# Activation columns held apart by parity, group norm pieces on GpSimd, and constant products ahead of the first matmuls in a two-convolution residual block

## The chip, the cores and the metric

The kernel runs on one core of a Trainium2 chip. A core has a matrix engine (TensorE; PE in the profile, its weight loads PEld), a vector engine (DVE), an activation engine (ACT), a general engine (GpSimd; POOL) and a queue that only starts transfers (SP). They run side by side and wait for one another through semaphores. The metric is the device time of one execution in microseconds, as a median over runs; lower is better.

## The reference

A residual block of a diffusion model, on two samples of 512 channels and 64 x 64 pixels, in bf16:

```python
def gn(z, gamma, beta):                    # 4 groups of 128 channels
    zr = z.reshape(B, G, (C // G) * H * W)
    mu = zr.mean(-1).reshape(B, G, 1)
    var = ((zr - mu) ** 2).mean(-1).reshape(B, G, 1)
    zn = ((zr - mu) / jnp.sqrt(var + eps)).reshape(B, C, H, W)
    return zn * gamma.reshape(1, C, 1, 1) + beta.reshape(1, C, 1, 1)
h = conv3(_silu(gn(x, g1, be1)), w1)       # 3x3, zero padding
emb = _silu(t_emb) @ w_emb
h = h + emb.reshape(B, C, 1, 1)
h = conv3(_silu(gn(h, g2, be2)), w2)
return x + h
```

## The kernel before, in words

**Tiles.** The 512 channels are four tiles of 128 partitions (index ct for inputs, ot for outputs). The pixels are cut into four chunks of 32 rows: chunk 0 and 1 are sample 0, chunk 2 and 3 sample 1. Each of the two layers (convolutions) runs over the four chunks, and each chunk over the four output tiles: 32 sets in all (`one_set`; the last one is `final_set`).

**Winograd along rows.** A convolution is not done tap by tap. Groups of 4 output rows are made from 6 positions: `make_v` builds six sums V of the activation rows, `u_blocks` six sums U of the weights, TensorE multiplies them (`row_pair`, three column taps each, 512 wide, eight groups of 64 columns), and the products are put together again on ACT and DVE (the m1, w and y lines of `one_set`). For positions 0 and 5 most chunks (`is_col`: all of layer 1, chunks 1 to 3 of layer 0) use a transform along columns too: `make_v` makes sums and differences of neighbouring columns into V, for which even and odd columns are taken out of a row with a step of 2, and `col_pair` multiplies by `u_cols` weights, 256 wide; outputs of even and odd columns come out apart and are written into y with a step of 2. The last two chunks of layer 1 do this for positions 1 and 3 as well (`more_cols`, `more_pair`, `v_more`, `v_more_split`).

**A row of activations** (tile a_tmp) has 66 places: a zero, 64 columns, a zero. `silu_rows` writes it from x (layer 0) or from h, the first layer's output, which goes out to memory and comes back (layer 1).

**Statistics.** `first_stats` (sample 0) uses TensorE: products of x blocks with themselves (L943), whose diagonal DVE sums (L333, acc with ident), and column sums. `second_stats` (sample 1) uses sums on DVE (L985) and squares on ACT. Layer 1 takes sums that the output instructions of layer 0 leave behind (`stats2`). `norm` makes scale (sc) and bias (nb) of silu: a matmul with ones (L405) sums over partitions, DVE copies it out (L409), small DVE instructions make the variance, POOL adds eps (L419) and takes the power -1/2 (L423), small DVE instructions finish.

**Order.** Nothing is issued in the order of the text. Every instruction is a node of a plan (`_Plan`) with a cost, a landing time for transfers (PARAM_LAND for the parameters) and a due time. The planner lists the nodes many times with random changes and keeps the best order; each engine then runs its own list strictly in order. So a changed cost or node can move instructions everywhere. All helpers issue from one line each: `tt` (sum of two tensors on DVE) is L320, `ts` L325, `stt` L333, `act` L350, `dma` L368, transposes L389, matmuls of `groups` L645.

**Buffers that the steps touch.** acc0 to acc2 are three PSUM accumulators of 2 x 512; m1, mb, sd, w are single SBUF tiles for evictions and their sums; y0 to y2 hold finished chunks; Vbuf has two sets of four, one per chunk in turn. A finished y of layer 1 gets x added by an accumulating transfer from the POOL queue and goes out through SP; the last set loads x into y beforehand and sends its result as two halves from SP and ACT.

Of the kernel before, what the change touches and what calls it, by code (L numbers as in the profile page):

```python
# [24 lines left out]
class _Plan:  # L25
# [33 lines left out]
    def region(self, a):  # L59
        if isinstance(a, str):  # L60
            return a, 1
        m = self.mask(a.offset, tuple((d[0], d[1]) for d in list(a.ap)[1:]))
        bank = self.banks.get(a.tensor.name)
        if bank:
            m = sum(1 << i for i in range(8) if (m >> (i * bank)) & ((1 << bank) - 1))
        return a.tensor.name, m
# [124 lines left out]
def kernel(  # L191
# [36 lines left out]
    PARAM_LAND = 5.5  # L228
    LATE = 4.0
    DVE_SUMS = (1,)  # L230
# [31 lines left out]
    neg_half = sb([1], "neg_half", F32)  # L262
# [134 lines left out]
    def norm(layer, b, c0, n, me, ps=None):  # L397
# [15 lines left out]
        if n == 1:  # L413
            stt(nvar[:], mu, mu, ex, ALU.mult, ALU.add)
        else:
            tt(nvar[:], mu, mu, ALU.mult)
            tt(nvar[:], nvar[:], ex, ALU.add)
        ts(nvar[:], nvar[:], 0.0, op=ALU.min)
        pool(lambda: nc.gpsimd.tensor_scalar(out=rstd[:], in0=nvar[:], scalar1=-1.0, scalar2=EPS,  # L419
                                             op0=ALU.mult, op1=ALU.add), [nvar[:]], [rstd[:]])  # L420
        for i in range(n):
            r = rstd[:, i:i + 1]
            pool(lambda r=r: nc.gpsimd.tensor_tensor(out=r, in0=r, in1=neg_half[:], op=ALU.pow), [r, neg_half[:]], [r])  # L423
        sc, nb = sc_all[layer, b][:, c0:c0 + n], nb_all[layer, b][:, c0:c0 + n]
        tt(sc, rstd[:], gam(layer)[:, c0:c0 + n], ALU.mult)
        if layer == 1:
            tt(mu, mu, emb_sb[:, b, c0:c0 + n], ALU.add)
        if n == 1:
            stt(nb, mu, sc, bet(layer)[:, c0:c0 + n], ALU.mult, ALU.add)
        else:  # L430
            tt(nb, mu, sc, ALU.mult)
            tt(nb, nb, bet(layer)[:, c0:c0 + n], ALU.add)
# [92 lines left out]
    def v_more(V, X):  # L525
        rows = lambda kx, st: view(V, kx, [[2 * NI, 2], [WP, TR], [st, W // st]])
        dst = lambda o, n: view(X, o, [[n * TR, 2], [n, TR], [1, n]])
        tt(dst(0, W), rows(0, 1), rows(2, 1), ALU.subtract)
        tt(dst(4 * NC, W // 2), rows(1, 2), rows(2, 2), ALU.add)
        tt(dst(6 * NC, W // 2), rows(2, 2), rows(1, 2), ALU.subtract)  # L530
# [3 lines left out]
    def v_more_split(V, at, D):  # L534
        rows = lambda kx, st: view(at, kx, [[NI, 2], [WP, TR], [st, W // st]])
        tt(view(D, 0, [[W * TR, 2], [W, TR], [1, W]]), rows(0, 1), rows(2, 1), ALU.subtract)
        dst = lambda i: view(V, i * 2 * NI, [[NC, 2], [W // 2, TR], [1, W // 2]])
        tt(dst(0), rows(1, 2), rows(2, 2), ALU.add)
        tt(dst(1), rows(2, 2), rows(1, 2), ALU.subtract)

    def rhs_more_split(V, D, j, c):
        if c in (0, 3):
            return view(D, j * 2 * NC + (1 if c == 3 else 0), [[W, TR], [2, W // 2]])
        return view(V, (c - 1) * 2 * NI + j * NC, [[1, NC]])

# [3 lines left out]
    def rhs_row(V, pos, kx, col):  # L549
        i = pos - 1 if col else pos  # L550
        return view(V, i * NI + kx, [[WP, TR], [1, W]])

    def rhs_col(V, j, c, o=4 * NI):
        if c in (0, 3):
            return view(V, o + j * 2 * NC + (1 if c == 3 else 0), [[W, TR], [2, W // 2]])
        return view(V, o + (4 if c == 1 else 6) * NC + j * NC, [[1, NC]])

    def silu_rows(layer, b, ch, ct, res, at):
# [3 lines left out]
        for edge, r in ((ch == 0, 0), (ch == NCH - 1, CR + 1)):  # L562
            if edge:
                pool(lambda r=r: nc.gpsimd.memset(rows[:, r, 1:W + 1], 0.0), [], [rows[:, r, 1:W + 1]], cost=0.2)  # L564
        act(rows[:, lo - r0:hi - r0, 1:W + 1], res[:, lo * W:hi * W].rearrange("p (r w) -> p r w", w=W)
            if res.shape[1] == HW else res.rearrange("p (r w) -> p r w", w=W),
            func=ACT.Silu, bias=nb_all[layer, b][:, ct:ct + 1], scale=sc_all[layer, b][:, ct:ct + 1])

    def make_v(V, at, rs, col, on_act, split=False):
# [25 lines left out]
        if split:  # L595
# [4 lines left out]
        tt(view(V, o, [[W, 2 * TR], [1, W]]), view(vt_, vo, [[WP, 2 * TR], [1, W]]),  # L600
           view(vt_, vo + 2, [[WP, 2 * TR], [1, W]]), ALU.subtract)
        odd = view(vt_, vo + 1, [[WP, 2 * TR], [2, W // 2]])
        evn = view(vt_, vo + 2, [[WP, 2 * TR], [2, W // 2]])
        tt(view(V, o + 4 * NC, [[W // 2, 2 * TR], [1, W // 2]]), odd, evn, ALU.add)
        tt(view(V, o + 6 * NC, [[W // 2, 2 * TR], [1, W // 2]]), evn, odd, ALU.subtract)
# [60 lines left out]
    def col_pair(cc, U, V, gid, lead=0.0, js=(0, 1)):  # L666
        a = next_acc()
        a4 = a[:].rearrange("p j (k n) -> p j k n", k=2)
        todo = []
        for j in js:  # L670
            for k, c in enumerate(cc):
                pairs = [(u_col(U[ct], j, c), rhs_col(V[ct], j, c)) for ct in range(CT)]
                todo.append(((j, k), a4[:, j, k], [t[0] for t in pairs], [t[1] for t in pairs], 0.11 * CT))
        groups(todo, a, (gid, cc, js), lead)
        return a4

    def more_cols(U, V, gid):
        def cols(cc):
            a = next_acc()
            a4 = a[:].rearrange("p j (k n) -> p j k n", k=2)  # L680
            todo = []
            for j in range(2):
                for k, c in enumerate(cc):
                    pairs = [(u_col_more(U[ct], j, c), rhs_more_split(V[ct], spare(ct), j, c)) for ct in range(CT)]
                    todo.append(((j, k), a4[:, j, k], [t[0] for t in pairs], [t[1] for t in pairs], 0.11 * CT))
            groups(todo, a, (gid, "more", cc))
            return a4
        act(mb[:].rearrange("p k j n -> p j k n"), cols((1, 2)), scale=0.5 * KAPPA)
        tt(sd[:, 0], mb[:, 0], mb[:, 1], ALU.add)
        tt(sd[:, 1], mb[:, 0], mb[:, 1], ALU.subtract)  # L690
        aa = cols((0, 3))
        for k, f in ((0, KAPPA), (1, -KAPPA)):
            stt(view(m1, k, [[NFREE, 2], [2, NC]]), aa[:, :, k], f, sd[:, k], ALU.mult, ALU.add)
# [18 lines left out]
    def more_pair(U, gid):  # L712
# [6 lines left out]
        out = lambda i: view(m1, i, [[NFREE, 2], [2, NC]])  # L719
        tt(par(0), comp(2), comp(3), ALU.add)  # L720
        tt(par(1), comp(2), comp(3), ALU.subtract)
        tt(out(0), par(0), comp(0), ALU.add)
        tt(out(1), par(1), comp(1), ALU.subtract)

    def final_set(U, V):
# [8 lines left out]
        act(mb[:].rearrange("p k j n -> p j k n"), a, scale=0.5)  # L734
        tt(sd[:, 0], mb[:, 0], mb[:, 1], ALU.add)
        tt(sd[:, 1], mb[:, 0], mb[:, 1], ALU.subtract)
        n = CR * W // 2
        y12, y03 = y4[:, 1:3], y4[:, 0:TH:TH - 1]
        both = lambda t, o: view(t, o, [[0, 2], [W, TR], [1, W]])
        tt(y12, y12, both(m1, 0), ALU.add)  # L740
        tt(y03, y03, both(m1, 0), ALU.add)
        for i in range(2):
            sd4 = sd[:, i].rearrange("p j (t w) -> p j t w", t=TR)
            tt(sd4, sd4, view(y, i, [[(TH - 1) * W, 2], [TH * W, TR], [2, W // 2]]), ALU.add)
        z = view(stage[1], 0, [[NFREE, 2], [1, NFREE]])
        e = view(stage[2], 0, [[NFREE, 2], [1, NFREE]])
# [7 lines left out]
        tt(y12, y12, t4(z), ALU.add)  # L754
        a = row_pair((2,), U, V, True, gid, 1)
        q = [view(vt, i * NFREE, [[1, NFREE]]) for i in range(3)]
        act(q[1], a[:, 0], scale=KAPPA)
        act(q[0], a[:, 0], scale=-KAPPA)
        act(q[2], a[:, 0], scale=-KAPPA)
        pm = lambda i: view(vt, i * NFREE, [[NFREE, 2], [1, NFREE]])  # L760
        tt(e, e, pm(1), ALU.add)
        tt(y12, y12, t4(pm(0)), ALU.add)
        aa = col_pair((0, 3), U, V, gid)
        for h in range(2):
            for k, op in ((0, ALU.add), (1, ALU.subtract)):
                part = lambda t: t.rearrange("p j (t w) -> p j t w", t=TR)[:, :, h * TR // 2:(h + 1) * TR // 2]
# [303 lines left out]
```

## Time and profile before

| What | Value |
|---|---|
| Median of 3 runs | 503.41 us (503.31 to 504.07) |
| The profiled execution | 503.6 us, of which span 501.7 |
| Busy in the span | PE 479.1, PEld 285.8, DVE 468.2, ACT 398.3, POOL 38.4 us |
| Clock of TensorE on the page | 1.00 up to 490 us, 0.80 from 490 to 501.7 |
| L645 PE 128x512 x1440, 128x256 x960 | mean 381 and 273 ns of one |
| L320 DVE sum, 128x1024 packed (w<-m,w) x62 | mean 683 ns |
| L320 DVE sum, 128x512 (y<-m,w) x62 | mean 416 ns |
| L320 DVE sum, 128x512 written with a step (m<-stage,vt) x8 | mean 729 ns |
| L950 DVE sum over 1024 elements of x, x2 | mean 1212 ns |
| L350 ACT silu, 128x2112 (a_tmp<-src) x20 | mean 2152 ns |
| L419, L423 POOL, 128x1, mean | 604, 713 ns |
| PE waits from 12.3 to 50 us | 3.2 us for V from DVE, 1.9 us for the diagonal sums |
| First silu (ACT) starts | 14.54 us |
| Diagonal sum of the first tile (DVE) | 10.58 us; the matmul behind it 11.55 |
| PE's last product ends, DVE's last sum ends | 494.2, 498.03 us |

The profile shows one execution. "Busy" of PE counts the overlapping lengths of its pipelined products; a product of 512 has a mean of 381 ns, but 27 of them in a row take 6.05 us (at 83.57 us). A wait is given as "who <- for whom: us in total, times, longest". The chain of waits is followed back from the last instruction: 51% of the span on PE, 18% on DVE, 5% on ACT; it lies on DVE from 112 to 209 us, on ACT from 232 to 257, and on PE from 257 to 491.

### The profile page before, as it was taken

How to read it: one execution, taken by the hardware profiler on the slowest of the kernel's cores; microseconds unless marked ns; L12 is line 12 of the kernel's file. 1: busy time of each engine (PE TensorE's matmuls, PEld its weight loads, DVE VectorE, ACT ScalarE, POOL GpSimd, SP SyncE). 2: the span in 40 equal slices, each digit the busy share in tenths (PEclk: the TensorE clock that was granted, in tenths of full speed). 3: DMA queues.
4: the chain of work that ended last, by engine and by line, in shares of the span. 5: the costliest groups of instructions: out<-in, count | busy, mean ns of one | idle time of the engine just before them, and what ended most of it. 6: DMA issues, size and time to landing. Idle time of an engine off the chain costs nothing.

```text
span 501.7 us, 8355 instructions
## 1 busy us (share of the span) xinstructions
PE 479.1 (95%) x3081; PEld 285.8 (57%) x3082; DVE 468.2 (93%) x1054; ACT 398.3 (79%) x548; POOL 38.4 (8%) x97
## 2 busy tenths in 40 slices
PE   5888999999999999999999999999999999999994
PEld 4654554455554555555665655555555666768572
DVE  3988999999999999899999999999999999998576
ACT  4888999999985895999999999767667867526362
POOL 1120000000110002000000000040010000000000
PEclk9999999999999999999999999999999999999998
DMA  8433233641210333222643122453626642424354
GB/s 301 178 77 92 69 106 121 220 181 43 78 51 2 109 105 110 86 86 89 179 137 114 67 86 51 120 129 84 171 43 151 187 125 47 127 62 107 85 125 127
DMA packets 17315, 55.53 MB, mean 111 GB/s; under 512 B 1915, under 2 KB 3067, under 8 KB 16507
## 3 DMA queue, kind: packets, MB, share of 16 engines
q1 hardware_dynamic: 14912, 46.86, 27.5%
q0 software_dynamic: 2160, 7.87, 9.5%
q8 instruction: 24, 0.39, 0.4%
q10 hardware_dynamic: 203, 0.27, 0.1%
q14 instruction: 16, 0.13, 0.1%
HBM read 38.22 MB, written 16.78 MB: 110 GB/s over the span
## 4 chain that ended last, share of the span: by engine, by line
PE 51%; DVE 18%; ACT 5%; POOL 1%; issue 1%; DVEq 0%
PE acc L645 50%; DVE V L320 4%; DVE vt L320 4%; DVE w L320 2%; DVE y L320 2%; DVE y L333 2%; ACT U L495 1%; POOL arena L423 1%; DVE sd L320 1%; DVE arena L985 1%; ACT a_tmp L350 1%; DVE vt L325 1%; PE xa L389 1%; ACT m L350 1%; POOL arena L419 1%
## 5 line engine op out<-in xcount | busy, mean ns | idle before, releaser
L645 PE MATMUL acc<-V,U 128*128 128x512 bf16 (+1 forms) x2400 | 435.1, 338 | 7.0 <-DVE V L320 3.2
L645 PEld LDWEIGHTS <-U 128*128 128x128 bf16 x2592 | 250.2, 98 | 186.2 <-issue 9.5
L320 DVE TENSOR_TENSOR V<-vt 128x1056 bf16<-128x1056 bf16 (+2 forms) x132 | 90.3, 691 | 3.6 <-ACT vt L350 1.2
L350 ACT ACTIVATE m<-w 128x512 bf16<-128x512 bf16 x62 | 38.1, 636 | 14.7 <-DVE w L320 14.6
L350 ACT ACTIVATE w<-acc 128x1024 bf16<-128x1024 f32 (+1 forms) x32 | 32.5, 1016 | 19.2 <-PE acc L645 7.8
L320 DVE TENSOR_TENSOR w<-m,w 128x1024 bf16<-128x1024 bf16 (+1 forms) x63 | 42.7, 679 | 5.0 <-ACT w L350 4.6
L350 ACT ACTIVATE src<-vt 128x528 bf16<-128x528 bf16 x54 | 34.6, 650 | 15.5 <-DVE vt L320 15.3
L320 DVE TENSOR_TENSOR U<-U 128x768 bf16<-128x768 bf16 (+2 forms) x96 | 45.1, 483 | 0.7 <-ACT U L495 0.5
L350 ACT ACTIVATE a_tmp<-src,arena 128x2112 bf16<-128x2112 bf16 x20 | 43.0, 2152 | 2.7 <-DVE stage L320 2.7
L350 ACT ACTIVATE mb<-acc 128x1024 bf16<-128x1024 f32 x32 | 32.8, 1024 | 12.4 <-PE acc L645 8.1
L320 DVE TENSOR_TENSOR vt<-a_tmp 128x1056 bf16<-128x1056 bf16 x56 | 39.0, 700 | 0.7 <-ACT a_tmp L350 0.4
L389 PEld LDWEIGHTS <-stage 128*128 128x128 bf16 x288 | 26.5, 144 | 12.5 <-DMA stage<-in_w_dram 3.8
L350 ACT ACTIVATE y<-y 128x2048 bf16<-128x2048 bf16 x16 | 30.6, 1909 | 0.0
L495 ACT COPY U<-xa 128x768 bf16<-128x768 bf16 x31 | 25.6, 826 | 3.8 <-PE xa L389 3.7
L320 DVE TENSOR_TENSOR sd<-mb 128x512 bf16<-128x512 bf16 x64 | 25.8, 417 | 2.4 <-ACT mb L350 2.4
L350 ACT ACTIVATE m<-acc 128x1024 bf16<-128x1024 f32 x24 | 24.6, 1025 | 3.4 <-DVE y L320 3.3
L350 ACT ACTIVATE a_tmp<-V,arena 128x2112 bf16<-128x2112 bf16 x12 | 26.0, 2169 | 1.6 <-DVE arena L333 1.6
L320 DVE TENSOR_TENSOR y<-m,w 128x512 bf16<-128x512 bf16 x62 | 24.7, 416 | 1.1 <-ACT m L350 0.7
L368 POOL DMA_DIRECT2D y<-in_x_dram x15 | 13.2, 879 | 149.6 <-DVE y L320 128.6
L564 POOL MEMSET a_tmp<- 128x64 bf16 x32 | 5.2, 167 | 241.3 <-DVE vt L320 213.9
L320 DVE TENSOR_TENSOR vt<-vt,a_tmp 128x1056 bf16<-128x1056 bf16 x32 | 22.4, 701 | 0.9 <-ACT vt L350 0.9
L350 ACT ACTIVATE src<-V 128x2048 bf16<-128x2048 bf16 x12 | 22.9, 1906 | 0.0
(115 smaller groups left out, 504.6 us busy)
## 6 DMA issues: line engine op xcount, KB each, us to landing
stage<-in_w_dram SPq DMA_DIRECT2D x32, 288.0 KB, 2.8
src<-h_scr SPq DMA_DIRECT2D x16, 528.0 KB, 3.8
h_scr<-y SPq DMA_DIRECT2D x16, 512.0 KB, 3.0
y<-in_x_dram POOLq DMA_DIRECT2D x15, 512.0 KB, 5.6
out_dram<-y SPq DMA_DIRECT2D x15, 512.0 KB, 2.9
V<-in_x_dram SPq DMA_DIRECT2D x6, 1024.0 KB, 6.8
src<-in_x_dram SPq DMA_DIRECT2D x4, 528.0 KB
V<-in_x_dram SPq DMA_DIRECT2D x4, 512.0 KB, 6.9
```

The source lines that it names most:

```text
L320: lambda: nc.vector.tensor_tensor(out=out, in0=in0, in1=in1, op=op), [in0, in1], [out], **kw)
L325: nc.vector.tensor_scalar(out=out, in0=in_, scalar1=c, scalar2=None, op0=op)
L333: nc.vector.scalar_tensor_tensor(out=out, in0=in0, scalar=scalar, in1=in1, op0=op0, op1=op1, **extra)
L350: nc.scalar.activation(out=out, in_=in_, func=fn, scale=scale, **extra)
L368: q.dma_start(out=out, in_=in_, **extra)
L389: nc.tensor.transpose(sel(t), in_, ident[:in_.shape[0], :in_.shape[0]])
L419: pool(lambda: nc.gpsimd.tensor_scalar(out=rstd[:], in0=nvar[:], scalar1=-1.0, scalar2=EPS, op0=ALU.mult, op1=ALU.add), [nvar[:]], [rstd[:]])
L423: pool(lambda r=r: nc.gpsimd.tensor_tensor(out=r, in0=r, in1=neg_half[:], op=ALU.pow), [r, neg_half[:]], [r])
L495: lambda: nc.scalar.copy(out=out, in_=sel(bank.get())), [tok], [out])
L564: pool(lambda r=r: nc.gpsimd.memset(rows[:, r, 1:W + 1], 0.0), [], [rows[:, r, 1:W + 1]], cost=0.2)
L645: nc.tensor.matmul(ap, lhsT=l, rhs=r, start=k == 0, stop=k == total[key] - 1)
L985: plan.add("DVE", 2.18, lambda xin=xin, o=part[:, k:k + 1]: nc.vector.reduce_sum(out=o, in_=xin, axis=AX.X), [xin], [part[:, k:k + 1]])
```

## The change

Four things are done.

1. **Columns apart.** A row of activations is now 33 even places and 33 odd ones (HP = 33). silu reads x with a step of 2 in layer 0; layer 0 writes h with even and odd columns apart, so layer 1 reads packed halves. The V sums of the column transform read packed runs of 32. `rhs_row` takes two runs of 32 for a tap. Sums and evictions (m1, sd, mb, accumulators) stay apart by parity. Natural order comes back when y is written in layer 1: rows 0 and 3 by DVE with a step as before, rows 1 and 2 by two ACT copies per set. The sum w03, added to y before, is added to sd.
2. **Fewer, larger sums.** The two sums into y rows 1 and 2 become one of 1024.
3. **Norm.** The power is taken over all columns at once; except for sample 0 of layer 0 and sample 1 of layer 1 ("quick") the small instructions move from DVE to POOL. `second_stats` adds its partial sums on POOL.
4. **Start.** 46 products of a tile of ones with itself, 22 bound to nothing but the ones, 24 to the first weights' landing, go to TensorE ahead of and between the first real ones. PARAM_LAND goes from 5.5 to 8.3.

`final_set` is rewritten to match: everything for rows 0 and 3 is collected in sd before the last column products arrive. The core of the diff:

```diff
@@ norm
+        def two(out, in0, in1, op, fast=False):
+            if fast:
+                tt(out, in0, in1, op)
+            else:
+                pool(lambda: nc.gpsimd.tensor_tensor(out=out, in0=in0, in1=in1, op=op), [in0, in1], [out])
+
+        quick = quick or (layer, b) == (1, B - 1)
+        two(nvar[:], mu, mu, ALU.mult, quick)
+        two(nvar[:], nvar[:], ex, ALU.add, quick)
...
+        pool(lambda: nc.gpsimd.tensor_tensor(out=rstd[:], in0=rstd[:], in1=nh, op=ALU.pow), [rstd[:], nh], [rstd[:]],
+             cost=0.7)
+        two(sc, rstd[:], g_, ALU.mult, quick)
...
+        two(nb, mu, sc, ALU.mult, quick)
+        two(nb, nb, b_, ALU.add, quick)
@@ rhs_row
-        return view(V, i * NI + kx, [[WP, TR], [1, W]])
+        o, step = ((0, HP), (HP, 1 - HP), (1, HP))[kx]
+        return view(V, i * NI + o, [[WP, TR], [step, 2], [1, HW2]])
@@ silu_rows
+        order = (HW2, [-HW2, 2], [1, HW2]) if layer == 1 else (1, [-1, 2], [2, HW2])
+        act(rows[:, lo - r0:hi - r0, 1:W + 1].rearrange("p r (k n) -> p r k n", k=2),
+            view(res, first + order[0], [[W, hi - lo]] + list(order[1:])),
@@ make_v
-        odd = view(vt_, vo + 1, [[WP, 2 * TR], [2, W // 2]])
-        evn = view(vt_, vo + 2, [[WP, 2 * TR], [2, W // 2]])
...
+        pairs = lambda i: view(vt_, vo + i, [[WP, 2 * TR], [HP, 2], [1, HW2]])
+        tt(view(V, o, [[W, 2 * TR], [HW2, 2], [1, HW2]]), pairs(0), pairs(1), ALU.subtract)
+        odd, evn = halves(vt_, vo + HP, 2 * TR), halves(vt_, vo + 1, 2 * TR)
@@ final_set
+        tt(e, e, both, ALU.add)
+        tt(flat(sd), flat(sd), e, ALU.add)
+        tt(z, z, both, ALU.add)
...
+        act(q[:, 0], a[:, 0], scale=KAPPA)
+        act(q[:, 1], a[:, 0], scale=-KAPPA)
...
+        act(nat(0), split, scale=-KAPPA)
+        act(nat(1), split, scale=KAPPA)
+        tt(flat(sd), flat(sd), q, ALU.add)
+        tt(y12, y12, t4(flat(vt, 2 * NFREE)), ALU.add)
@@ one_set
-        tt(y4[:, 1], z12[:, 0], t4(w_[:, 1, 0:1])[:, 0], ALU.add)
-        tt(y4[:, 2], z12[:, 1], t4(w_[:, 0, 0:1])[:, 0], ALU.add)
+        if layer == 0:
+            tt(y4[:, 1:3], t4(m1[:]), s1t1, ALU.add)
+        else:
+            tt(t4(m1[:]), t4(m1[:]), s1t1, ALU.add)
+            for f in range(2):
+                act(view(yst, (1 + f) * W, [[TH * W, TR], [1, 2], [2, HW2]]),
+                    m1[:, f].rearrange("p (t k w) -> p t k w", k=2, w=HW2))
...
+                flat = view(sd, 0, [[NFREE, 2], [1, NFREE]])
+                tt(flat, flat, w_[:, :, 0], ALU.add)
@@ start
-    PARAM_LAND = 5.5
+    PARAM_LAND = 8.3
+    WARM = (11, 12)
...
+    for after in [()] * WARM[0] + [(wload[0][:, 0:1],)] * WARM[1]:
+        plan.add("PE", 0.2, lambda: [nc.tensor.matmul(acc[2][:, 1, 0:P], lhsT=ones_bf[:], rhs=ones_bf[:], start=True,
+                                                      stop=True) for _ in range(2)],
+                 [ones_bf[:]] + list(after), [acc[2][:]], group=("warm",), lat=0.1, due=4.0, lead=-100.0)
...
-        norm(0, 0, ct, 1, me, ps=st[:, 0, 0:2])
+        norm(0, 0, ct, 1, me, ps=st[:, 0, 0:2], quick=True)
@@ second_stats
-        stt(me[:, 0:1], part[:, 0:1], 1.0, part[:, 1:2], ALU.mult, ALU.add)
-        ts(me[:, 0:1], me[:, 0:1], 1.0 / HW)
-        tt(me[:, 1:2], part[:, 2:3], part[:, 3:4], ALU.add)
+        pair = me[:, 0:2]
+        pool(lambda: nc.gpsimd.tensor_tensor(out=pair, in0=part[:, 0:4:2], in1=part[:, 1:4:2], op=ALU.add),
+             [part[:, 0:4]], [pair])
```

## The prediction

> **What bounds the kernel now.** I read first the busy times by stage, cut where the behaviour changes. The columns are the stretch and its length in us, then for each engine its busy us and, in brackets, its instructions.
>
> ```profile
> 0.00:12.30 12.30, 6.44 (x54) 5.67 (x55) 4.23 (x16) 5.44 (x7) 2.39 (x26) 1.00 0.83 298
> 12.30:50.00 37.70, 31.95 (x278) 20.64 (x278) 33.79 (x96) 31.31 (x43) 5.26 (x12) 1.00 0.38 118
> 50.00:112.00 62.00, 61.78 (x360) 31.07 (x359) 61.02 (x126) 61.64 (x94) 0.62 (x4) 1.00 0.42 141
> 112.00:209.00 97.00, 95.23 (x552) 53.37 (x550) 94.76 (x245) 81.34 (x111) 10.36 (x21) 1.00 0.22 75
> 209.00:257.00 48.00, 46.59 (x308) 27.96 (x307) 45.02 (x99) 46.82 (x70) 0.62 (x4) 1.00 0.36 112
> 257.00:322.00 65.00, 64.92 (x414) 38.04 (x414) 64.66 (x157) 62.11 (x91) 1.52 (x4) 1.00 0.32 97
> 322.00:490.00 168.00, 167.99 (x1102) 106.86 (x1100) 156.90 (x306) 106.18 (x133) 16.83 (x26) 1.00 0.43 108
> 490.00:501.70 11.70, 4.19 (x25) 2.22 (x23) 7.79 (x18) 3.43 (x6) 0.81 (x1) 0.80 0.49 135
> ```
>
> In order PE, PEld, DVE, ACT, POOL: PE is busy 167.99 of 168 us from 322 to 490, so a faster DVE or ACT is worth nothing there. All that can be had lies in the idle time of PE: the first 50 us, a little from 112 to 257, and the tail. The waits of PE between 50 and 325 us say how much the middle holds:
>
> ```profile
> PE acc L645 <- DVE y L333: 1.8, 2, 1.1
> PE acc L645 <- ACT mb L350: 1.4, 2, 0.8
> PE acc L645 <- ACT m L350: 0.2, 1, 0.2
> ```
>
> That is 3.4 us in all. The 1.8 us fall at 151 and 209, and 0.6 of ACT's 1.4 at 136; in this stage DVE is busy 94.76 of 97 us and carries the chain of waits (ACT's own part there: 81.34 of 97). The other 0.8 come at 256, where the chain runs on ACT.
>
> **The change, part by part.**
>
> *Strided reads on DVE.* The profile's groups, shapes kept apart (busy us, mean ns of one, idle before):
>
> ```profile
> L350 ACT ACTIVATE m<-w 128x512 bf16<-128x512 bf16 x62 | 38.1, 636 | 14.7 <-DVE w L320 14.6
> ...
> L320 DVE TENSOR_TENSOR V<-vt 128x512 bf16<-128x512 bf16 x48 | 32.4, 682 | 0.0
> L320 DVE TENSOR_TENSOR sd<-mb 128x512 bf16<-128x512 bf16 x64 | 25.8, 417 | 2.4 <-ACT mb L350 2.4
> ```
>
> The same 512 sums take 682 ns where both inputs step over every second element (V) and 417 ns where everything is packed (sd). With even and odd columns apart the V sums become packed: 265 ns less each. 72 such sums exist (48 into V from vt, 24 with a_tmp, src and V in the last chunks): 72 x 0.265 = 19.1 us of DVE. From 112 to 209 lie 16 of them (4.2 us), from 50 to 112 eight, from 12 to 50 none, since the first chunk is computed without column transforms. The eight m<-stage,vt (729 ns, written with stride) become packed too, after 322.
>
> *Fewer instructions on DVE.* Two 512 sums y<-m,w (mean 416) become one of 1024 (683 as w<-m,w): 31 x 0.15 = 4.6 us, 0.9 of it (six pairs) from 112 to 209. The norm of sample 1 (layer 0) and sample 0 (layer 1) goes to POOL: 28 + 7 small instructions of about 0.15 us (arena rows, 143 to 213 ns), against 8 more in the first norms; some 26 of them lie between 112 and 209: 3.9 us. So that stage loses 4.2 + 0.9 + 3.9 = 9.0 us of DVE work, against 2.4 us of PE waits that DVE causes. PE is then the bound, and more than 2.4 cannot come of it. I take 2.0 (bounds 0 and 2.4), because each wait also hangs on the order of DVE's queue. Everything saved from 50 to 112, where PE is busy 61.78 of 62, and after 322 lies beside PE and is costed at nothing.
>
> *Norm on POOL.* Behind the statistics' matmul there are now eight POOL instructions in a row, of which POOL did two before. POOL's rows between 112 and 145 run from 0.19 to 1.76 us, mean 0.72; eight make 5.8 us, plus 0.08 between each, 6.4. Before, the last norm took from DVE's copy at 141.19 to the bias at 147.66, 6.5 us, because its small pieces queued between DVE's large ones. About even: 0, bounds from the smallest and largest row (8 x 0.19 to 8 x 1.76), -5 to +8 us on this chain. POOL's queue holds only its memsets beside it (10.36 us busy of 97), and what waits behind is the silu of the same tile on ACT, then DVE's V, then PE. The norm of sample 0 in layer 1 swaps four powers in a row (2.98 us of the chain from 198.41) for one over four columns, and takes six small ones more: about even as well.
>
> *Constant products at the start.* This view of the timeline has start, length, engine, line, tiles and count:
>
> ```profile
> 8.58 1.89 PE L943 MATMUL acc<-V 128*128 128x128 bf16 x16
> ...
> 12.29 1.95 PE L943 MATMUL acc<-V 128*128 128x128 bf16 x32
> ```
>
> Sixteen products take as long at 8.6 us as thirty-two at 12.3: TensorE runs at half speed before, though the page prints a full clock (1.00) there. It was busy 3.7 us on end (8.5 to 12.3) when the change came; the burst from 5.4 to 7.3 was not enough. The change gives it 46 products of ones; the first 22 wait only for a memset (DVE 0.98), 10 for the first weights (landed 3.78), the rest stand around the first statistics, so it works almost without a break from 1.2 to 8, twice as long as was needed. The second half of x lands at 8.6 either way (ACT waits for it until 8.62). Its 16 products then take about 1.0 instead of 1.89. DVE's sum over x (1.21 us) ends at 9.8, so the diagonal sum starts there instead of 10.58, the copy that stood behind it is moved away, the statistics' matmul goes from 11.55 to about 10.6, and its fp32 pass takes 0.38 (row at 18.84) instead of 0.59: 1.1 us earlier, less two small DVE instructions that replace one, twice (0.3). First silu 0.8 us earlier; bounds 0 (clock not raised) and 1.1. The ten products in front of the first transposes delay them by 10 x 0.11 = 1.1 us; DVE, which copies them, idles from about 6 to 8.7, so this costs nothing, and 1.1 if that idle time were gone. The parameters' transpose (L916) moves behind the statistics; it waited until 8.45 beside the same landing: nothing.
>
> *The rest of the first 50 us.* DVE gets no relief there, and PE's waits (3.2 us for V, 1.9 for the diagonal sums) stay. The order on PE, DVE and ACT is a new one: 0, bounds -2 to +2.
>
> *Strided reads and copies on ACT.* Sixteen silus of layer 0 read every second element; 30 copies of 128x512 bring natural order into the outputs of layer 1, written with stride. No row shows ACT with a stride in SBUF. From below 0, from above DVE's ratio 682/417 = 1.64. ACT already takes (2152 - 636)/(2112 - 512) = 0.95 ns for an element, where DVE's packed sum takes 0.52: it is nearest to an engine with no pairing to lose, so I take 0. The copies by the row m<-w are 30 x 0.64 = 19 us. 22 of them lie after 322, beside 62 us of idle ACT: nothing. They also hold m1 about 1.3 us longer; the next eviction into m1 is behind them on the same engine, and PE has three accumulators: nothing, or 15 x 1.3 = 20 us if PE ran dry each time. Eight lie in 257 to 322: 5.1 us against 2.9 idle. I take +0.5, since silus of later chunks can move past 322; bounds 0 and 5.1 - 2.9 = 2.2.
>
> *Matmuls.* Row products now read two runs of 32 instead of one of 64. The column products read every second element for c = 0 and 3 and packed for 1 and 2, all in one group of 273 ns: the pattern costs nothing. 0.
>
> *Tail.* Before, DVE did 3.8 us of work after PE's last product (494.2 to 498.03), the outputs' landing 3.6 more. Now the column products come last, and the row products are evicted 1.8 us (16 products) sooner by four ACT instructions (2.1 us). I lay out DVE's queue from the last eviction but one: seven sums before the first column sum, then four column sums (0.36 each) and one of 0.6, ends 3.4 us after PE's last product. Gain 0.4; bounds -0.4 and 1.0.
>
> Sum: -0.8 - 2.0 + 0.5 - 0.4 = -2.7 us. The profiled execution took 503.6 (span 501.7 and 1.9 around it), so 500.9; the median is 0.2 lower, so 500.7.
>
> **The rivals.**
>
> *A: packing fails for the odd starts.* The new V operands start at an odd element (33 or 1). No row shows a packed sum that starts odd. If such a sum ran like a strided one, the 72 sums stay at 682, and the 32 differences of 1024 for c = 0 and 3, packed before, would go from 0.68 to 1.21 (DVE's sum over 1024 elements of x, one by one, x2 in the profile). From 112 to 209 that is 8 x 0.53 = 4.2 us, which eats the 0.9 + 3.9; no wait of PE goes away. From 257 to 322 three of them add 1.6 to a DVE that has 0.34 us free: +1.0. Time: 503.4 - 0.8 - 0.4 + 0.5 + 1.0 = 503.7, no change. 8%.
> [...]
>
> *B, slower: POOL's norm chain decides.* Place: the last norm of sample 1, from about 140. PE's wait at 151 already hangs on V made from it. For: one POOL instruction took 1.76 us there:
>
> ```profile
> 142.84 1.76 POOL L419 TENSOR_SCALAR arena<-arena 128x1 f32<-128x1 f32 x1 [1.69 <-DVE arena L325]
> ```
>
> At 1.76 each, eight take 14.7 with the gaps instead of 6.5: 8.2 later, less 3 that DVE's relief upstream gives: +5, and the 2.0 are lost: 503.4 - 0.7 + 5 = 507.7. It decides from about 1.1 us per instruction (6.5 + 2.7 = 8 x 1.07 + 0.64). Against: the other seven rows are 0.19 to 1.02. 9%.
> [...]
>
> *C, slower: ACT pays for the stride.* 4 silus each in 12 to 50 and in 50 to 112 (ACT busy 61.64 of 62), 1.4 us each: +5.5 in the second alone, 506. Against: 0.95 ns per element. 4%.
>
> *D: the constant products raise no clock and the new order brings no fewer waits:* 503.4 + 0.5 - 0.4, no change. 5%.
>
> **How the numbers follow.** The forecast has 74%, and its own range is 497.5 to 502.3 (start -1.1 to 0, first stages -2 to +2, waits -2.4 to 0, ACT 0 to 2.2, tail -1.0 to +0.4, not all at one end). A measurement of this kernel can tell about 0.2%, 1.0 us. Faster: the forecast less its upper edge, and parts of A and D, 0.76. Same: 0.10. Slower: B, C and an edge of D, 0.14. The range 496.8 to 503.6 leaves out about 7% below (a new order that also mends the waits before 50 us) and 13% above.
>
> **What would show it.** V<-vt 128x512 at 417 ns (682: A). Grams of 16 in about 1.0 us at 8.6, first silu near 13.7. PE's waits from 50 to 325 near 1.4 us and on ACT, not DVE. POOL's small rows under 1.1 us. Eight copies y<-m at 0.64 and ACT full from 257 to 322. The silu rows still 2152. I would be wrong if 27 row products took more than the 6.05 us of the row at 83.57, or if PE waited longer before 50 us than the 5.1 us now.

## The result, and the profile after

The kernel after takes 509.3 us (507.66 to 510.06, four runs); the kernel before took 503.36 us beside it. The ratio is 1.0112, 95% interval 1.0082 to 1.0141: slower by 5.9 us, where 2.7 us less was forecast. The profiled execution took 508.68 us, its span is 506.9.

The first view is the busy time by stage of the kernel after, cut where the kernel before was cut: stretch and length, then busy us and instructions of PE, PEld, DVE, ACT and POOL, then TensorE's clock, the share of the transfer engines and GB/s.

```profile
0.00:12.30 12.30, 8.98 (x114) 8.40 (x115) 4.88 (x20) 5.44 (x7) 3.35 (x28) 1.00 0.84 310
12.30:50.00 37.70, 33.58 (x269) 21.38 (x269) 33.27 (x100) 32.50 (x47) 5.09 (x11) 0.95 0.40 122
50.00:112.00 62.00, 62.00 (x342) 29.07 (x341) 58.48 (x113) 57.83 (x88) 1.79 (x6) 1.00 0.42 145
112.00:209.00 97.00, 97.00 (x551) 53.46 (x550) 92.40 (x208) 86.05 (x113) 23.92 (x54) 1.00 0.19 65
209.00:257.00 48.00, 48.00 (x308) 28.15 (x306) 42.15 (x99) 45.52 (x67) 0.78 (x5) 1.00 0.34 110
257.00:322.00 65.00, 65.00 (x411) 37.18 (x410) 61.94 (x133) 60.60 (x87) 2.46 (x5) 1.00 0.34 96
322.00:490.00 168.00, 167.31 (x1088) 105.67 (x1086) 153.96 (x313) 127.52 (x164) 13.43 (x22) 1.00 0.43 112
490.00:506.90 16.90, 9.08 (x56) 5.35 (x55) 10.61 (x23) 6.55 (x11) 0.86 (x1) 0.89 0.36 93
```

PE is busy for every one of the 272 us from 50 to 322; before, it idled there now and then. DVE has 92.40 us of work from 112 to 209 where it had 94.76. So PE's idle time in the middle, which the change aimed at, is gone, and still the end is later. The sum of PE's busy time is 491.0 us where it was 479.1. Its waits on the row and column products in the whole span:

```profile
PE acc L664 <- DVE V L323: 2.7, 6, 0.8
...
PE acc L664 <- DVE y L323: 0.6, 1, 0.6
PE acc L664 <- ACT mb L353: 0.2, 1, 0.2
```

Those of DVE y and ACT mb fell from 3.2 to 0.8 us; of the 2.7 us for V, 2.3 lie before 50 us and 0.4 after 322. With hardly a wait left, a later end means that PE's own work became longer. The groups with shapes kept apart (busy us, mean ns of one, idle before) show where. First the row products of the kernel before, then the kernel after:

```profile
L645 PE MATMUL acc<-V,U 128*128 128x512 bf16 x1440 | 336.6, 381 | 7.0 <-DVE V L320 3.2 <-DVE y L333 1.8 <-ACT mb L350 1.4
```

```profile
L664 PE MATMUL acc<-V,U 128*128 128x512 bf16 x1440 | 343.9, 389 | 2.9 <-DVE V L323 2.7 <-ACT mb L353 0.2
...
L664 PE MATMUL acc<-V,U 128*128 128x256 bf16 x960 | 117.3, 272 | 0.6 <-DVE y L323 0.6
L353 ACT ACTIVATE a_tmp<-src,arena 128x2112 bf16<-128x2112 bf16 x20 | 42.8, 2142 | 2.5 <-DVE arena L323 2.4
...
L353 ACT ACTIVATE a_tmp<-V,arena 128x2112 bf16<-128x2112 bf16 x12 | 25.7, 2144 | 3.1 <-DVE arena L323 2.8 <-POOL arena L423 0.4
...
L323 DVE TENSOR_TENSOR sd<-mb 128x512 bf16<-128x512 bf16 x64 | 24.5, 419 | 2.7 <-ACT mb L353 2.5
...
L353 ACT ACTIVATE y<-m 128x512 bf16<-128x512 bf16 x30 | 21.3, 764 | 0.4 <-DVE m L323 0.3
...
L323 DVE TENSOR_TENSOR V<-vt 128x512 bf16<-128x512 bf16 x48 | 19.6, 434 | 0.1
...
L323 DVE TENSOR_TENSOR V<-vt 128x1024 bf16<-128x1024 bf16 x24 | 17.3, 720 | 0.1
```

The row products have a mean of 389 ns where it was 381. That looks like little, but the lengths overlap: the step from one product to the next is much shorter. A run of products in the timeline (start, length, engine, line, count) shows this pace, before and after:

```profile
83.57 6.05 PE L645 MATMUL acc<-V,U 128*128 128x512 bf16 x27
```

```profile
69.07 12.37 PE L664 MATMUL acc<-V,U 128*128 128x512 bf16 x54
```

Take off the last product's length, 0.39 us, and divide the rest by the steps between starts: (12.37 - 0.39) / 53 = 226 ns for each product. The row of the kernel before gives (6.05 - 0.38) / 26 = 218 ns. Eight more ns on 1440 row products are 11.5 us. The single starts in these two rows say which tap it is: before, the next product starts 215 or 216 ns after an outer tap and 222 or 223 after a middle one; after, 221 or 222 and 233 to 236.

### The profile page after: what moved, and what is told of

It is laid out like the page before. It is cut to its first block, busy times and chain, and to the rows that moved or that the text cites. A ratio compares the mean times of both kernels' runs of the same rounds, so it can differ in the third digit from the quotient of the medians.

```text
span 506.9 us, 8510 instructions
## 1 busy us (share of the span) xinstructions
PE 491.0 (97%) x3126; PEld 288.7 (57%) x3128; DVE 457.7 (90%) x1000; ACT 422.0 (83%) x579; POOL 51.7 (10%) x130
## 4 chain that ended last, share of the span: by engine, by line
PE 83%; DVE 10%; ACT 3%; DMA 2%; issue 2%; POOL 0%; DVEq 0%; ACTq 0%
PE acc L664 79%; DVE V L323 3%; PE xa L392 2%; DMA V<-in_x_dram 1%; DVE y L323 1%; DVE sd L323 1%; DVE w L323 1%; PE xb L392 1%; ACT m L353 1%; DVE vt L323 1%; PE acc L982 1%; ACT mb L353 1%; DMA stage<-in_w_dram 1%; DVE U L323 1%; DVE m L336 1%
## 5 line engine op out<-in xcount | busy, mean ns | idle before, releaser
L664 PE MATMUL acc<-V,U 128*128 128x512 bf16 (+1 forms) x2400 | 444.1, 342 | 3.5 <-DVE V L323 2.7
L323 DVE TENSOR_TENSOR V<-vt 128x1056 bf16<-128x1056 bf16 (+2 forms) x132 | 77.4, 609 | 3.0 <-ACT vt L353 1.2
L353 ACT ACTIVATE a_tmp<-V,arena 128x2112 bf16<-128x2112 bf16 x12 | 25.7, 2144 | 3.1 <-DVE arena L323 2.8
L323 DVE TENSOR_TENSOR sd<-mb 128x512 bf16<-128x512 bf16 x64 | 24.5, 419 | 2.7 <-ACT mb L353 2.5
L371 POOL DMA_DIRECT2D y<-in_x_dram x15 | 13.3, 887 | 128.3 <-DVE y L323 46.7
L323 DVE TENSOR_TENSOR w<-w 128x1024 bf16<-128x1024 bf16 x31 | 21.4, 690 | 2.8 <-ACT w L353 0.9
```

The costliest lines, as they stand in the source:

```text
L323: lambda: nc.vector.tensor_tensor(out=out, in0=in0, in1=in1, op=op), [in0, in1], [out], **kw)
L353: nc.scalar.activation(out=out, in_=in_, func=fn, scale=scale, **extra)
L371: q.dma_start(out=out, in_=in_, **extra)
L664: nc.tensor.matmul(ap, lhsT=l, rhs=r, start=k == 0, stop=k == total[key] - 1)
```

## The experiments

**Theory:** TensorE takes longer to stream a moving operand that is read as two runs of 32 per row, because of where the runs start. **Rivals:** the new order, the copies on ACT, the norm on POOL, or the constant products and what the clock does after them.

**e1: products alone.** One loop of 48 products for each pattern, for instance (shortened)

```python
for j in range(48):   # as the middle tap of the kernel after
    matmul(acc, lhsT=w, rhs=view(x, 33, [[66, 8], [-32, 2], [1, 32]]))
```

> A kernel of products alone: 48 matmuls in a row for each pattern in which TensorE can read its moving operand, each pattern on a line of its own and twice over, with nothing else running. It computes none of the reference. Theory (the read pattern costs): rows of 64 that start at an even element 48 x 0.216 = 10.4 us, rows that start at an odd one 10.7, the halves at 0 and 33 (one even, one odd) 10.7, the halves at 33 and 1 (both odd, read backward) 11.3, flat reads of 512 the same 10.4 at either start. If only the start's parity counts, the halves at 34 and 2 take 10.4, at 1 and 35 some 11.0, at 33 and 0 10.7; if the backward step counts, 34 and 2 take 10.7 or more. Rival (the longer spacing in the kernel comes from other engines reading the same memory, or from the clock): every pattern of 512 takes the same 10.4.

The timeline of this kernel, one row for each pattern:

```profile
31.31 10.52 PE L45 MATMUL acc<-xt,wt 128*128 128x512 bf16 x48
41.67 10.84 PE L47 MATMUL acc<-xt,wt 128*128 128x512 bf16 x48
52.35 10.84 PE L49 MATMUL acc<-xt,wt 128*128 128x512 bf16 x48
63.03 11.37 PE L51 MATMUL acc<-xt,wt 128*128 128x512 bf16 x48
74.23 10.88 PE L53 MATMUL acc<-xt,wt 128*128 128x512 bf16 x48
...
106.61 10.52 PE L59 MATMUL acc<-xt,wt 128*128 128x512 bf16 x48
116.97 11.16 PE L61 MATMUL acc<-xt,wt 128*128 128x512 bf16 x48
...
170.82 5.40 PE L71 MATMUL acc<-xt,wt 128*128 128x256 bf16 x48
176.06 5.60 PE L73 MATMUL acc<-xt,wt 128*128 128x256 bf16 x48
```

L45 and L47 are the rows of 64 of the kernel before, from place 0 (outer taps) and from place 1 (middle tap). L49 is the outer tap after (halves at 0 and 33), L51 its middle tap (33, then 1). L53 reads halves at 34 and 2, L59 at 0 and 34, L61 at 1 and 35. L71 reads 256 packed, L73 every second element. From 40 to 170 us no other engine is busy and the clock is 1.00 (0.999 as a mean of the whole run), so other engines and the clock are no explanation here. An outer tap costs (10.84 - 10.52) / 48 = 6.7 ns more, a middle tap (11.37 - 10.84) / 48 = 11.0. With 960 and 480 of them: 6.4 + 5.3 = 11.7 us. Two runs of 32 are not slow as such (L59 is as fast as L45); eight odd starts cost 6.7 ns (L47, L49), sixteen 13.3 where each run begins just behind the last (L61) and 17.7 where the second lies before the first (L51). A read with a step of 2 costs (5.60 - 5.40) / 48 = 4.2 ns more.

**e2 and e3: the read alone, in both kernels.** Both edits leave every instruction and the order on each engine as they are; the traces show the same order on PE, DVE, ACT and POOL as in the kernel that each starts from. So the new order, the copies, the norm and the constant products are all still in e2, and none of them is in e3.

```diff
 # e2, in the kernel after
-        return view(V, i * NI + o, [[WP, TR], [step, 2], [1, HW2]])
+        return view(V, i * NI + kx, [[WP, TR], [1, W]])
 # e3, in the kernel before
-        return view(V, i * NI + kx, [[WP, TR], [1, W]])
+        return view(V, i * NI + (0, WP // 2, 1)[kx], [[WP, TR], [(WP // 2, 1 - WP // 2, WP // 2)[kx], 2], [1, W // 2]])
```

> The kernel after, but its row products read one run of 64 at the column offset, as in the kernel before; every other instruction and the order on every engine stay. The row products pick the wrong columns. Theory (the read pattern costs): by the matmuls' spacing 960 products x 6.2 ns + 480 x 12.8 ns = 12.1 us come back, about 497 us. Rival (the new order of the instructions, the copies on ACT, the norm on POOL or the constant products cost the time): 509, as the kernel after.

> The kernel before, but its row products read two runs of 32 in the pattern of the kernel after; every other instruction and the order on every engine stay. The row products pick the wrong columns. Theory (the read pattern costs): +12 us on the stretches in which TensorE is the bound, less the 3.4 us of its waits between 50 and 322 us that it can soak up: 512 to 515 us. Rival (something else in the change costs the time): 503.4, as the kernel before.

e2 took 500.31 us (498.88 to 501.92), ratio to before 0.9933 (0.9916 to 0.995): 9.0 us less than the kernel after. e3 took 511.83 us (511.53 to 513.16), ratio 1.0173 (1.016 to 1.0186): 8.5 us more than the 503.31 of the kernel before beside it. The same run of 27 products that took 6.05 us in the kernel before, in e3, and the row products as a group, in e2 and in e3:

```profile
85.27 6.27 PE L645 MATMUL acc<-V,U 128*128 128x512 bf16 x27
```

```profile
L664 PE MATMUL acc<-V,U 128*128 128x512 bf16 x1440 | 332.4, 382 | 4.2 <-DVE V L323 3.0 <-DVE y L336 0.4 <-DVE U L323 0.3
```

```profile
L645 PE MATMUL acc<-V,U 128*128 128x512 bf16 x1440 | 348.0, 388 | 5.3 <-DVE V L320 4.2 <-DVE y L333 0.5 <-DVE arena L409 0.2
```

The read decides the sign, in both directions: with it the row products' busy time goes from 332.4 to 343.9 us in the one kernel and from 336.6 to 348.0 in the other, 11.5 and 11.4 us, as the products alone say. The time moves by less. In e3, PE's whole busy time grows by 10.6 us (479.1 to 489.7) and its idle time falls by 2.2, since slower products wait less; together they are the 8.4 by which the span is longer. In e2 the new waits lie in a stage that the prediction left out:

```profile
322.00:490.00 168.00, 164.76 (x1084) 105.72 (x1083) 152.75 (x313) 125.55 (x164) 14.27 (x23) 1.00 0.43 108
```

PE idles 3.2 us there, where it idles 0.7 in the kernel after and had no idle time in the kernel before; 2.2 of it waits for y from DVE, 0.9 for V. These 2.5 us more and the 9.0 between the medians are the 11.5. The sum fits less well between the two profiled executions, which differ by 6.8 us: that of e2 (501.92) is the slowest of its six.

**e4: V moved by one element.** Even columns then start at 1 and odd ones at 34: the middle tap reads from 34 and 2, both even, the outer taps still one odd and one even half.

```diff
+    VO = 4 * NI + 2
...
-        return view(V, i * NI + o, [[WP, TR], [step, 2], [1, HW2]])
+        return view(V, i * NI + 1 + o, [[WP, TR], [step, 2], [1, HW2]])
...
-    def rhs_col(V, j, c, o=4 * NI):
+    def rhs_col(V, j, c, o=VO):
```

> The kernel after with the row positions of V moved by one element, so that even columns start at an odd element and odd columns at an even one: the middle tap then reads two even starts (34 and 2), the outer taps one of each as now. The matrix of ones lies in another tile's space, and V is two elements longer. Theory, parity of the start alone: the middle taps go from 235 to 216 ns, 480 x 19 = 9 us less, about 500. Theory, parity and the backward step: 235 to 222, 6 us less, about 503. Rival (not the read): 509.

506.44 us (505.47 to 507.15), ratio to before 1.006: 2.9 us less than the kernel after. Both forecasts are missed, the nearer one, 503, by 3.4. The prices of products alone explain it afterwards: the middle tap gains (11.37 - 10.88) / 48 x 480 = 4.9 us, and the column operands in V, which now start two elements later, lose by e10 below (5.56 - 5.40) / 48 x 448 = 1.5 us (448 products read a packed half from V: 28 sets with a column transform, 16 each). Net 3.4. The groups of its trace agree: the row products' busy time falls from 343.9 to 339.2 us, that of the column products from V rises from 117.3 to 118.7.

**e10: what beside the odd start costs.** Runs of 32 at pitch 64, started at 0, 1, 2, 4, 8 (L45 to L53, 256 wide), at 2 and at 1 (L65, L67, 512 wide), and backward pairs that start at 32 and 0 (L69).

> Products alone once more, 48 in a row for each pattern, each pattern on two lines; it computes none of the reference. It asks what beside the odd start costs time. Theory 1 (runs of 32 read whole lines, and a line that isn't the next one costs extra): runs of 32 at pitch 64 take 5.4 us for 48 of 256 when they start at 0 or 32, and some 5.5 when they start at 2, 4, 8 or 16; at 1 they take 5.7. Backward pairs that start on whole lines take no more than forward ones, 10.5. Theory 2 (the backward step itself costs): backward pairs take 10.9 wherever they start, and all even starts take 5.4.

```profile
31.66 5.40 PE L45 MATMUL acc<-xt,wt 128*128 128x256 bf16 x48
36.90 5.73 PE L47 MATMUL acc<-xt,wt 128*128 128x256 bf16 x48
42.47 5.56 PE L49 MATMUL acc<-xt,wt 128*128 128x256 bf16 x48
47.87 5.44 PE L51 MATMUL acc<-xt,wt 128*128 128x256 bf16 x48
53.15 5.40 PE L53 MATMUL acc<-xt,wt 128*128 128x256 bf16 x48
...
99.94 10.94 PE L65 MATMUL acc<-xt,wt 128*128 128x512 bf16 x48
110.72 11.36 PE L67 MATMUL acc<-xt,wt 128*128 128x512 bf16 x48
121.92 10.52 PE L69 MATMUL acc<-xt,wt 128*128 128x512 bf16 x48
163.84 21.84 PE L77 MATMUL acc<-xt,wt 128*128 128x512 bf16 x48
```

Neither theory as written: the backward step costs nothing (L69, 10.52 us), and a start at 8 elements is as good as one at 0 (5.40 us each), at 4 nearly so (5.44); at 2 a product of eight runs costs 3.3 ns more, at 1 6.9. So runs that do not follow on one another were free here when they started on 8 elements, 16 bytes; and L67, forward from 1, takes as long as the middle tap in e1 (11.36 and 11.37), so what makes that tap dearer than L61 there (11.16) is the gap between its runs and not the step back. The whole lines of theory 1 were its author's supposition: it had some 5.5 us for a start at 8, where 5.40 was measured, and no run shows lines. A read of every fourth element took twice as long as the runs of 32 of L69 (L77, 21.84 us against 10.52, 512 wide).

**e9: the columns' read alone, in the kernel before.**

```diff
-            return view(V, o + j * 2 * NC + (1 if c == 3 else 0), [[W, TR], [2, W // 2]])
+            return view(V, o + j * 2 * NC + (W // 2 if c == 3 else 0), [[W, TR], [1, W // 2]])
```

> The kernel before, but the column products for c = 0 and 3 read a packed half instead of every second element; every other instruction and the order on every engine stay. These products pick the wrong columns. Theory (a read of every second element costs too, 113.4 ns against 109.1 in the kernel of products alone): 572 x 4.3 ns = 2.5 us less where TensorE is the bound, 500.9. Rival (column products cost the same in both patterns, as the mean of their group says): 503.4.

502.85 us (501.67 to 503.48, 11 runs), ratio 0.9981 (0.9972 to 0.9991): 0.8 us less. The direction is the theory's, the size a third of it. The edit reaches 512 products, not 572 (448 from V and 64 of the last chunk), which makes 2.1 us, and PE's busy time falls by 1.9 (479.1 to 477.2). Its idle time takes part of that back: from 112 to 257 us, where DVE and ACT set the pace, PE is busy 94.85 and 46.34 us where it was 95.23 and 46.59.

**e5, e7, e11, e12: the constant products.** e5 is the kernel after without them. e7 and e12 are the same kernel: the one before with the norm on POOL, the merged sums and the constant products, in the old layout; e11 adds 16 constant products near 21 us. Unlike e2, e3, e4 and e9, these kernels and e6 and e8 are planned anew, so their differences hold a new order too.

```diff
 # e5, in the kernel after
-    WARM = (11, 12)
+    WARM = (0, 0)
 # e11, in first_stats of e7, tile 2, ahead of norm
+    FILL = 8
...
+            for _ in range(FILL):
+                plan.add("PE", 0.2, lambda: [nc.tensor.matmul(acc[0][:, 1, 0:P], lhsT=ones_bf[:], rhs=ones_bf[:], start=True,
+                                                              stop=True) for _ in range(2)],
+                         [ones_bf[:], Ut[0][0][2][:, S_G2, :]], [acc[0][:, 1, 0:P]], group=("fill",), lat=0.1, lead=900.0)
```

> The kernel after without its 46 constant products; the planner orders the rest anew. The trace of the kernel after shows TensorE at full clock from 4.7 us, but at half speed again from 21.8 to 25.2 us; the kernel before has no such stretch. Theory (the early full clock is paid back by that stretch): the start is 0.8 us later, the 3.4 us at half speed, worth 1.7 us of products, are gone, 508.4. Rival (the stretch has another cause, or lies beside other waits): 509.3 + 0.8 = 510.1.

e5: 509.09 us (508.47 to 510.6), as the kernel after. Its first silu starts at 14.8 us where that of the kernel after starts at 13.26, 1.5 us later (the kernel before has 14.54). In e5 sixteen products still take 1.91 us at 14.03, half speed, and thirty-two take 1.95 at 18.16. The kernel after is at full speed from 4.74 us, but a later window shows a loss:

```profile
21.80:25.20 3.40, 3.40 (x24) 2.55 (x25) 2.80 (x12) 2.43 (x3) 0.79 (x2) 0.50 0.35 92
```

TensorE runs at half speed (0.50) for 3.4 us while it is busy throughout, worth 1.7 us of products (an estimate, half of 3.4); once e5 is at full speed, it has no such stretch before its end (the clock by stage is 1.00 up to 500 us). e5 lies between its theory (508.4) and the rival (510.1), so it does not decide. The single executions hint at the same size: in the kernel after, the one with a mean granted clock of 0.997 took 507.66 us, the three with 0.993 took 508.68 to 510.06; in e2, the three with 0.995 or more took 498.88 to 499.37, the three with 0.994 or less 501.25 to 501.92. Where the clock fell is known for the profiled executions alone.

> The kernel before with norm, merged sums and constant products, as in the earlier run, and 16 constant products more near 21 us, where TensorE waits before it falls back to half speed. Theory (the fall back comes from TensorE's idle time just before): no stretch at half speed near 24 us, 3.4 us x half = 1.7 less, 499.1. Rival (it comes for another reason, or the 16 products stand in the way): 500.8 or more.

> The kernel before with norm, merged sums and constant products, beside the run with 16 products more on the same chip: 500.8 as before, half speed again from about 24 to 27 us. If the stretch at half speed comes and goes from one execution to the next, the times spread over 1.7 us or more.

e11: 502.43 us (500.71 to 503.92), e12 beside it 501.38 (500.22 to 503.99). In e11's profiled execution TensorE keeps full speed near 22 us, as the theory has it (sixteen products at 23.86 take 1.05 us), and falls to half at 159.59 us instead, after a wait of 2.62 us for V that the new order has there. The 3.4 us ahead of the fall, in the kernel after and in e11 (the first figure after the length is PE's busy time):

```profile
18.40:21.81 3.41, 1.76 (x19) 1.35 (x19) 3.29 (x13) 3.41 (x7) 1.38 (x3) 1.00 0.31 85
```

```profile
156.17:159.59 3.42, 1.23 (x6) 0.58 (x6) 3.32 (x7) 2.27 (x3) 0.00 (x0) 1.00 0.37 153
```

PE was busy for 52% and 36% of it. In every profiled execution with such a fall it was 55% or less; but the kernel before had a stretch at 50% (1.70 of 3.41 us from 40.70) and e8 one at 55% (1.87 of 3.41 from 19.15), and both kept full speed (1.00), so a share like these alone does not bring the fall, and what else decides stays open. In time e11 is no gain: its rival holds. In e12, which spreads over 3.8 us, executions with a mean granted clock of 0.994 or more took 500.22 to 501.70 us, those with 0.992 or less 501.09 to 503.99.

**e6, e7, e8: the norm on POOL.**

```diff
 # e8, on top of e2
-        quick = quick or (layer, b) == (1, B - 1)
+        quick = True
 # e6 and e7, in one_set, beside norm and second_stats of the kernel after
-        tt(y4[:, 1], z12[:, 0], t4(w_[:, 1, 0:1])[:, 0], ALU.add)
-        tt(y4[:, 2], z12[:, 1], t4(w_[:, 0, 0:1])[:, 0], ALU.add)
+        tt(y4[:, 1:3], t4(m1[:]), s1t1, ALU.add)
```

> The kernel before with two parts of the change alone: the norm of the later tiles on POOL, and the two sums of 512 into y as one of 1024. The layout stays the old one, no constant products. Theory (PE's waits on DVE from 112 to 209 go once DVE has less to do): 0.9 + 3.9 = 4.8 us off DVE against 2.4 us of waits, 2.0 gained, 501.3. Rival (eight POOL instructions in a row delay the last tiles of sample 1 as much): 503.3 or more.

> The run before this one in the list, and the constant products with it. Theory (the ones bring the first silu 0.8 us forward and nothing else): 0.8 less than that run, 500.5 if it takes 501.3. Rival (the full clock lapses once more near 22 us, as in the kernel after): 0.9 more than that run, 502.2.

> The kernel after with the read of the kernel before (row products pick the wrong columns), and the norm on DVE in all places, its power on POOL. Theory (the norm on POOL is about even, and the packed sums alone take PE's waits away): 500.3, as with the norm on POOL. Rival 1 (DVE's 3.9 us more from 112 to 209 bring the waits back): 502.3. Rival 2 (the chain on POOL costs time): 498.

e6: 501.72 us (499.25 to 502.79), ratio 0.9957 (0.9942 to 0.9971), 2.0 us less, the theory's number. The place is not the theory's: in its trace PE is busy 95.65 us from 112 to 209, where it was 95.23; more comes from 209 to 257 (48.00 where it was 46.59) and from 12 to 50 (33.41 where it was 31.95), which the new order can give as well. e7: 500.76 (500.29 to 501.31), ratio 0.9945 (0.9933 to 0.9957); e12 repeats it with 0.9954 (0.9941 to 0.9967). Both beat the two kernels; between e6 and e7 the intervals overlap, so the ones' share is not settled. e8 took 507.25 us (505.9 to 509.22), 7 more than e2; rival 1 has the direction, neither has the size. The stage from 112 to 209, first in e2, then in e8:

```profile
112.00:209.00 97.00, 96.61 (x568) 55.51 (x567) 94.17 (x218) 87.90 (x116) 24.62 (x55) 1.00 0.21 70
```

```profile
112.00:209.00 97.00, 94.82 (x550) 53.61 (x549) 92.76 (x239) 83.63 (x110) 10.07 (x20) 1.00 0.21 75
```

1.8 us of PE's time are lost here, as rival 1 said. Some 1.1 more are lost from 322 to 490 (PE 164.76 and 163.64 us) and 0.8 from 12 to 50 (33.57 and 32.82). The order is another one throughout, so even the 1.8 is not the norm's alone; the two profiled executions differ by 4.9 us, and the rest of the 7 is not traced.

## Why the prediction was wrong

**The step that failed is "Matmuls".** It said of the row products' two runs of 32 that "the pattern costs nothing", from a group of column products with two patterns and one mean of 273 ns, and put the term at 0. Row products cost 11.7 us more by the products alone and 11.4 to 11.5 in the two kernels; with the read put back, e2 takes 500.3 us, where 500.7 was forecast for the whole. The inference was wrong twice: one mean over both patterns does not compare them (alone they differ by 4% in pace, L71 and L73, though their means of 272 and 274 ns differ by 0.7%), and the column pattern tells nothing of odd starts. The kernel before had a sign of it that was not looked for: its middle taps already start at an odd element, and its trace has 222 or 223 ns behind them where the outer ones have 215 or 216. The closing sentence of the prediction, on 27 products taking more than 6.05 us, named the very row that gave it away (6.27 in e3). No rival named the read; the two that were slower, B and C, were about other things.

**Strided reads on DVE:** right. The V sums run at 434 ns (417 forecast, 682 before), though they start at an odd element, so rival A, which had 682, is out. A little is left: sd, with even starts, has 419 ns on the same page, and the differences of 1024 went from 681 to 720. With odd starts these sums stayed within 4 to 6% of 417 and 681 ns.

**Fewer instructions on DVE, 2.0 us:** right for the stages it names. In the kernel after, slower products help to hide the waits, so e2 is the fair witness: PE's idle time from 112 to 322 falls from 3.3 us to 0.5. What the packed sums and the fewer instructions each do is not separated; e6, without the new layout, has the number in the wrong place. "After 322 lies beside PE and is costed at nothing" was wrong: at the old pace of the products PE loses 3.2 us there (e2). Neither e6 nor e7, with the old layout, loses as much there (0.9 and 0.3), and ACT has its copies in that stage (125.55 us busy where it was 106.18); but the order differs too, and the cause was not traced.

**Norm on POOL, 0:** no loss, so rival B is out: its instructions of 112 to 150 us have medians of 0.24 to 0.95 us, and e2, where PE has its old pace, idles 0.4 us in that stage. That it is worth nothing is not shown: back on DVE and in another order (e8) the time rose by 7 us, of which 1.8 lie in the stage in question.

**Constant products, -0.8:** the gain at the start was larger. Sixteen products took 1.07 us at 7.90, and the first silu starts at 13.26 us, 1.3 earlier than before. The half speed from 21.8 to 25.2 us, which the step on the first 50 us did not hold, takes 1.7 of it back, an estimate from its length and PE's busy time there; e5 takes 0.2 us less than the kernel after, so the sum is near zero as far as two different orders can say.

**ACT:** silu is as fast with a stride (2144 ns in the twelve of layer 0 that read V, 2169 before), so rival C is out; that ACT has no pairing to lose was the author's supposition, which no run shows. The copies that write with a step took 764 ns, not 640; ACT had 60.60 us of work in 65 from 257 to 322, and PE was busy throughout (65.00, and 64.85 in e2), so the 0.5 was not needed there.

**Tail, -0.4:** DVE's last sum ends at 503.24 us, 3.7 after PE's last product at 499.53 (3.8 before). 0.1 of the 0.4 is there.

**Column products, 0:** their packed reads are worth 576 x 4.2 ns = 2.4 us of PE's work by e1; e9, with 512 of them, shows 1.9 in PE's work and 0.8 in the time of the kernel before. This term was mis-sized in the other direction. With it, that e2 comes within 0.4 us of the forecast is luck: the columns' gain stands against the half speed and the 3.2 us after 322, none of which the sum held. In rival A, 1.6 less 0.34 is 1.3, not 1.0; nothing hangs on it.

## What to carry to other kernels

A layout that suits one engine is read by others too. Before moving columns, list each reader of the new layout with the start of every run it reads: for TensorE's bf16 operands in e1 and e10, starts on 8 elements (5.40 us for 48, as from 0), or runs that follow on one another from an even start (10.52: L45 and L59 of e1), were free; odd starts cost 0.8 ns a run (L47 and L61 of e1), and 1.1 in L51, whose runs do not follow on one another. When TensorE is the bound, judge a change by the pace of a run of products (length of the run over its count), not by a mean that puts patterns together. Take the parts of a change apart: here the norm on POOL and the merged sums alone, in the order that the planner then chose, give a kernel of 501.7 us, faster than both.

## What the runs showed that was not expected

- **Odd starts.** Eight runs at an odd element add 6.7 ns to a product of 512 that takes 216, sixteen add 13.3 though each run begins just behind the last; a single flat read from place 1 adds 0.8 (10.56 against 10.52 us for 48).
- **Half speed for one stretch**, in the kernel after of 3.41 us from 21.81, 17.07 us after full speed began at 4.74; e2, e4, e7 and e12 fell at 23.29, 22.24, 23.91 and 23.20 us, e11 at 159.59. In the kernel before, e5, e6 and e8 the clock by stage is 1.00 up to 490 us; the mean clock of e3 and e9, 0.997 and 0.996, is no lower than the 0.995 of the kernel before. PE was busy for 36 to 55% of the 3.41 us ahead of each fall; the cause is not shown.
- **ACT paid for a strided write, not for a strided read:** 764 ns (y<-m) against 624 (m<-w) for 512 elements, while silu with a step of 2 in its input takes 2144 ns, 2169 before.
